# Grouped-query attention with a gated MLP, one decode step: slots at multiples of 512 bytes, the extra w_out rows on other DMA engines, the side table inside the MLP rows

## The chip, the cores and the metric

The kernel runs on one core of a Trainium2 chip. The time is the device time of one execution in microseconds (us); lower is better. A core has five instruction streams (PE for matmuls, DVE for vector work, ACT for activations, POOL, and SP, which here only issues DMAs) and sixteen DMA engines that carry all its transfers.

## The reference, cut to what matters

```python
xn = _layernorm(x)                                   # x: 8 x 1 x 512
q = (xn @ wq) ...                                    # 32 heads of 128
scores = einsum("bhqd,bhkd->bhqk", q, k) * (Dh ** -0.5)   # k_cache: 8 x 8 x 4096 x 128
o = einsum("bhqk,bhkd->bhqd", softmax(scores), v)    # v_cache: the same shape
s = o @ wo                                           # 4096 x 512
z = gelu(xn @ w_in); z1, z2 = z[:896], layernorm(z[896:])
g = silu((z1 * (w_sp * z2 + b_sp)) @ w_out)          # w_out: 896 x 512
return x + s * g
```

All is float32. The two caches are 134 MB each; each KV head serves four query heads. Nothing is reused across batches, so every byte of the caches is read once.

## The kernel before, in words

SBUF holds three large buffers, the slots of the pool `ring`: each is 128 partitions by 64 KB (8.4 MB). Everything large passes through them in turn. SP issues in this order: the MLP's weights into the first slot (`w_mlp`, L70, then three small transfers `w_low`, L75), `wq` into the second (L86), then for each of the 8 KV heads two halves of K (`load_k`, L313) and two halves of V (`load_v`, L320), one slot each, and around the last half of V the output weights `wo` in seven pieces (L324). A load into a slot waits on SP until the compute that read the slot's last content has ended. A full slot is one DMA with one row of 64 KB for each partition; an engine carries eight of them.

The pool `const` is allocated ahead of `ring` in each partition, so the sizes of its tiles set where the slots start. In this kernel the slots start at bytes 16,704, 82,240 and 147,776 of a partition.

**The MLP.** `w_out` has 896 rows, seven blocks of 128. Five of them (`MAIN`) lie in `w_mlp`, one row for each partition and block, and so come over all engines. The other two blocks, 1 and 3 (256 rows of 2 KB), come in the three transfers of the list `LOW`. An entry `(e, p0, c0, chunks)` is one DMA whose source has `e` outer rows and whose destination is `4 * e` partitions from `p0`, with the given chunks of w_out's rows side by side in the columns from `c0`. Each outer row of the source becomes four packets, one for each of its four partitions. In `mlp()` each chunk takes one transpose of the activations (L201), a DVE copy for all chunks of the same height in a group of up to four (L206), and matmuls (L215); entries at `p0 > 0` accumulate in the second PSUM bank.

**The start.** ACT issues `x` (8 rows of 2 KB, L64) and the side table (`side`, 128 rows of 520 bytes, L66: x in the layout of the output, and the two scalars w_sp and b_sp). DVE and POOL normalise x (L129 to L133), PE transposes it (L136), and the MLP's first matmuls (L155) wait for `w_mlp`. The scalars are read at L186, the copy of x by the last addition at L383.

**Attention.** For each head PE computes the scores of both halves of K (L258), softmax follows, and `values` multiplies by V (L300), with the reduction on DVE (L303, L305). At the end `wo` is multiplied as its pieces land (L331, L338), the result is gated and x added (L382, L383), and SP writes it out (L384).

Of the kernel before, what the change touches and what calls it, by code (L numbers as in the profile page):

```python
# [8 lines left out]
F32 = mybir.dt.float32  # L9
# [4 lines left out]
P = 128  # L14
B, D = 8, 512
HKV, REP, S, DH = 8, 4, 4096, 128
NK = D // P
G = 4
J = S // (G * P)
R = 32  # L20
FH = 896
# [12 lines left out]
MAIN = [0, 2, 4, 6, 5]  # L34


def rows_of(j, lo, hi, n):
    return [(j, r) for r in range(lo, hi, n)]


LOW = [(2, R, 2 * D, rows_of(3, 0, P // 2, 8)), (4, 0, 2 * D, rows_of(1, 0, P, 16)),
       (8, 0, 0, rows_of(3, P // 2, P, 32))]
LOW_COLS = 10 * D
HL_AT = [0, 0, 8]
HL_CH = 10


@with_exitstack
def tile_gqa_gmlp_decode(ctx: ExitStack, tc: tile.TileContext, x, side, kT, v, wq, wo,
                         w_mlp, lows, out):  # L50
    nc = tc.nc
    const = ctx.enter_context(tc.tile_pool(name="const", bufs=1))
# [3 lines left out]
    ps_fix = ctx.enter_context(tc.tile_pool(name="ps_fix", bufs=1, space=bass.MemoryType.PSUM))  # L56
    ps = ctx.enter_context(tc.tile_pool(name="ps", bufs=2, space=bass.MemoryType.PSUM))

    def slot():
        return ring.tile([P, SLOT], F32, name="slot")  # L60


    x_sb = const.tile([B, D], F32, name="x_sb")
    nc.scalar.dma_start(x_sb, x)  # L64
    side_sb = const.tile([P, P + 2], F32, name="side_sb")
    nc.scalar.dma_start(side_sb, side)  # L66

    mlp_slot = slot()
    n_in, n_mlp = NK * 2 * FH, NK * 2 * FH + len(MAIN) * D
    nc.sync.dma_start(mlp_slot[:, :n_mlp], w_mlp)  # L70
    w_in_sb = mlp_slot[:, :n_in].rearrange("p (k n) -> p k n", k=NK)
    low_sb = []
    for (e, p0, c0, chunks), w_low in zip(LOW, lows):
        t = mlp_slot[p0:p0 + e * LOW_R, n_mlp + c0:n_mlp + c0 + len(chunks) * D]
        nc.sync.dma_start(t, w_low[:, :LOW_R * len(chunks) * D].rearrange("e (i n) -> e i n", i=LOW_R))  # L75
        low_sb.append(t.rearrange("p (c d) -> p c d", d=D))
    w_out_sb = mlp_slot[:, n_in:n_mlp].rearrange("p (j d) -> p j d", d=D)
    spare = [n_mlp + LOW_COLS]

    def from_slot(rows, n):  # L80
        lo = spare[0]
        spare[0] = lo + n
        return mlp_slot[:rows, lo:lo + n]

    wq_sb = slot()
    nc.sync.dma_start(wq_sb, wq)  # L86
    wq_sb = wq_sb.rearrange("p (k n) -> p k n", k=NK)
# [49 lines left out]
    nc.vector.tensor_copy(xnT[:, :, :B], pt.rearrange("p (k b) -> p k b", k=NK))  # L137

    gate = const.tile([P, P], F32, name="gate")

    def mlp():
        zu = work.tile([P, 4, FQ], F32, name="zu", tag="p")
# [2 lines left out]
        hT = hy[:, :2 * P].rearrange("p (a s) -> p a s", a=2)  # L145
        hL = from_slot(P, HL_CH * P).rearrange("p (a s) -> p a s", s=P)
        y_sb, e = zu[:, :2].rearrange("p a f -> p (a f)"), zu[:, 2, :P]
# [45 lines left out]
        todo = [(0, hT[:, j % 2, R * (j // 2):R * (j // 2 + 1)], w_out_sb[:, i, :]) for i, j in enumerate(MAIN)]  # L193
        for (ne, p0, _, chunks), c0, w_low in zip(LOW, HL_AT, low_sb):
            n = ne * LOW_R
# [115 lines left out]
    def load_k(h, half):  # L311
        t = slot()
        nc.sync.dma_start(t, kT[h, half])  # L313
        return t.rearrange("p (i c g s) -> p i c g s", i=HALF, c=2, g=G)
# [65 lines left out]

    res = const.tile([P, P], F32, name="res")
    nc.vector.tensor_mul(res, acc, gate)  # L382
    nc.vector.tensor_add(res, res, side_sb[:, :P])  # L383
    nc.sync.dma_start(out, res)  # L384


# [43 lines left out]
```

## Time and profile before

| | |
|---|---|
| median of 3 runs | 684.03 us (683.95 to 684.05) |
| the profiled execution | 683.97 us |
| its span, first to last instruction | 682.2 us |
| busy: PE, DVE, ACT, POOL | 382.8, 170.5, 13.5, 3.9 us |
| mean rate read from HBM over the span | 426 GB/s |
| SP's DMA queue q1 | 6262 packets, 290.79 MB, 98.8% of 16 engines |
| instruction fetches, q8 and q14 | 20 packets with 0.33 MB, 3 with 0.02 MB |

The profile is of one execution, and its span is 1.8 us shorter than the time of the same execution. A row of waits names who ended an engine's idle time; a row of the chain gives a start, a length and what was being waited for, followed back from the last instruction. The trace also holds a record for every DMA packet: queue, start, length and bytes, but not the engine.

### The profile page before, as it was taken

How to read it: one execution, taken by the hardware profiler on the slowest of the kernel's cores; microseconds unless marked ns; L12 is line 12 of the kernel's file. 1: busy time of each engine (PE TensorE's matmuls, PEld its weight loads, DVE VectorE, ACT ScalarE, POOL GpSimd, SP SyncE). 2: the span in 40 equal slices, each digit the busy share in tenths (PEclk: the TensorE clock that was granted, in tenths of full speed). 3: DMA queues.
4: the chain of work that ended last, by engine and by line, in shares of the span. 5: the costliest groups of instructions: out<-in, count | busy, mean ns of one | idle time of the engine just before them, and what ended most of it. 6: DMA issues, size and time to landing. Idle time of an engine off the chain costs nothing.

```text
span 682.2 us, 5712 instructions
## 1 busy us (share of the span) xinstructions
PE 382.8 (56%) x2610; PEld 117.5 (17%) x2610; DVE 170.5 (25%) x272; ACT 13.5 (2%) x27; POOL 3.9 (1%) x11
## 2 busy tenths in 40 slices
PE   1488454456655355556754465655755356655666
PEld 0222121112111021111211021111211021111212
DVE  2531033401431024401431024401422024400432
ACT  0000000000000000000000000000000000000000
POOL 1000000000000000000000000000000000000000
PEclk9778667878767678887676678877667778876688
DMA  9999999999999999999999999999999999999996
GB/s 384 439 447 432 434 431 430 428 434 428 438 435 430 431 430 435 438 428 430 428 434 443 427 439 439 431 434 431 430 431 430 430 431 428 430 431 434 424 422 263
DMA packets 6445, 291.22 MB, mean 427 GB/s; under 512 B 726, under 2 KB 982, under 8 KB 1534
## 3 DMA queue, kind: packets, MB, share of 16 engines
q1 hardware_dynamic: 6262, 290.79, 98.8%
q8 instruction: 20, 0.33, 0.2%
q10 hardware_dynamic: 160, 0.08, 0.1%
q14 instruction: 3, 0.02, 0.0%
HBM read 290.80 MB, written 0.07 MB: 426 GB/s over the span
## 4 chain that ended last, share of the span: by engine, by line
DMA 79%; PE 16%; issue 4%; DVE 1%; POOLq 0%; POOL 0%
DMA slot<-in_kT 40%; DMA slot<-in_v 28%; DMA slot<-in_wo 10%; PE sc L258 8%; PE o_ps L300 6%; PE sc L215 1%; PE scr L201 0%; PE po_ps L309 0%; DMA x_sb<-in_x 0%; DVE zu L218 0%; DVE st L129 0%; PE scr L191 0%; POOLq L424 0%; POOL rstd L132 0%; PE sc L338 0%
## 5 line engine op out<-in xcount | busy, mean ns | idle before, releaser
L258 PE MATMUL sc<-slot,qz 128*32 128x512 f32 x1024 | 148.0, 743 | 132.1 <-DMA slot<-in_kT 132.1
L300 PE MATMUL o_ps<-slot,pT 128*16 128x512 f32 x1024 | 154.0, 744 | 77.8 <-DMA slot<-in_v 77.8
L303 DVE TENSOR_TENSOR o_all<-o_ps,diag 128x512 f32<-128x512 f32 x64 | 44.2, 691 | 156.7 <-PE o_ps L300 156.3
L263 DVE TENSOR_REDUCE nm<-sc 128x1 f32<-128x1024 f32 x8 | 9.8, 1224 | 278.7 <-PE sc L258 278.7
L258 PEld LDWEIGHTS sc<-slot,qz 128*32 128x32 f32 x1024 | 36.5, 133 | 237.3 <-DMA slot<-in_kT 138.1
L305 DVE TENSOR_REDUCE o_sb<-o_all 128x128 f32<-128x512 f32 x64 | 67.8, 1059 | 2.2
L300 PEld LDWEIGHTS o_ps<-slot,pT 128*16 128x16 f32 x1024 | 30.5, 113 | 161.6 <-issue 106.9
L309 PE MATMUL po_ps<-fold,o_sb 128*128 128x4 f32 x128 | 24.6, 263 | 24.1 <-DVE o_sb L305 23.8
L309 PEld LDWEIGHTS po_ps<-fold,o_sb 128*128 128x128 f32 x128 | 19.0, 188 | 68.8 <-DVE o_sb L305 65.5
L289 PE MATMUL scr<-ident,p 128*128 128x128 f32 x64 | 15.4, 422 | 10.7 <-DVE p L284 10.7
L265 ACT ACTIVATE p<-sc,nm 128x1024 f32<-128x1024 f32 x8 | 8.9, 1113 | 574.5 <-DVE nm L263 574.5
L289 PEld LDWEIGHTS scr<-ident,p 128*128 128x128 f32 x64 | 12.4, 221 | 11.1 <-issue 11.1
L290 DVE COPY pT<-scr 128x512 f32<-128x512 f32 x16 | 11.1, 691 | 11.3 <-PE scr L289 11.3
L155 PE MATMUL scr<-slot,xnT 128*32 128x256 f32 (+1 forms) x64 | 5.2, 464 | 9.5 <-DMA slot<-in_w_mlp 9.5
L236 PE MATMUL scr<-slot,xnT 128*32 128x512 f32 x64 | 9.4, 737 | 0.0
L268 PE MATMUL scr<-ident,nm 128*1 128x128 f32 x8 | 2.2, 270 | 10.9 <-DVE nm L263 10.9
L281 PE MATMUL scr<-wl,same 128*128 128x1 f32 x16 | 3.8, 309 | 6.2 <-DVE wl L279 6.2
L284 DVE TENSOR_SCALAR p<-p,w 128x1024 f32<-128x1024 f32 x8 | 6.0, 753 | 0.3
L331 PE MATMUL sc<-slot,oT 128*8 128x512 f32 x48 | 5.7, 593 | 0.2 <-DMA slot<-in_wo 0.2
L215 PE MATMUL sc<-slot 16*32 16x512 f32 (+2 forms) x36 | 5.3, 664 | 0.8 <-DVE zu L218 0.8
L171 PE MATMUL scr<-part_sum,same 128*128 128x1 f32 x4 | 1.1, 348 | 7.0 <-DVE part_sum L169 7.0
L155 PEld LDWEIGHTS scr<-slot,xnT 128*32 128x32 f32 x64 | 3.0, 141 | 11.3 <-issue 10.8
(87 smaller groups left out, 72.3 us busy)
## 6 DMA issues: line engine op xcount, KB each, us to landing
slot<-in_v SPq DMA_DIRECT2D x2, 4096.0 KB, 26.3
slot<-in_w_mlp SPq DMA_DIRECT2D x1, 4864.0 KB, 14.5
slot<-in_wo SPq DMA_DIRECT2D x1, 3072.0 KB, 36.5
slot<-in_wo SPq DMA_DIRECT2D x1, 2048.0 KB, 40.1
slot<-in_wo SPq DMA_DIRECT2D x1, 1280.0 KB, 42.7
slot<-in_wo SPq DMA_DIRECT2D x1, 768.0 KB
slot<-in_wo SPq DMA_DIRECT2D x1, 512.0 KB
slot<-in_wo SPq DMA_DIRECT2D x2, 256.0 KB, 31.8
```

The lines of the kernel that those rows point to most:

```text
L155: nc.tensor.matmul(pz[R * g:R * (g + 1), part * FQ:part * FQ + n], xnT[:, k, :], w_in_sb[:, k, part * FH + lo:part * FH + lo + n], start=( ...
L215: nc.tensor.matmul(sc[R * g:R * (g + 1), bank, :], lhsT, rhs, start=(i < G), stop=(i + G >= len(part)))
L236: nc.tensor.matmul(pq[R * g:R * (g + 1), :], xnT[:, k, :], wq_sb[:, k, lo:lo + REP * DH], start=(k == 0), stop=(k == NK - 1))
L258: nc.tensor.matmul(sc[R * g:R * (g + 1), c, :], qz[:, h, b * R:(b + 1) * R], k_sb[:, i, c, g, :], start=(b == 0), stop=(b == B - 1))
L263: nc.vector.tensor_reduce(m, sc, op=ALU.max, axis=AX.XY, negate=True)
L265: nc.scalar.activation(p.rearrange("p j s -> p (j s)"), sc.rearrange("p c s -> p (c s)"), AF.Exp, bias=m, accum_out=l[:, h:h + 1])
L289: nc.tensor.transpose(t[:, j * P:(j + 1) * P], p[:, 4 * c + j, :], ident)
L290: nc.vector.tensor_copy(pT[:, :, 4 * c:4 * c + 4].rearrange("p b j (g r) -> p (j g) b r", g=G), t.rearrange("p (m b r) -> p m b r", b=B, r ...
L300: nc.tensor.matmul(of[R * c:R * c + G * REP, :], pT[:, b, j, :], v_unit[:, j], start=(j < G), stop=(j >= J - G))
L303: nc.vector.tensor_mul(o_all, o, diag[:, :, None].to_broadcast([P, G, DH]))
L305: nc.vector.tensor_reduce(o_sb, o_all.rearrange("p g d -> p d g"), op=ALU.add, axis=AX.X)
L309: nc.tensor.matmul(po[:, b * REP:(b + 1) * REP], o_sb, fold, start=True, stop=True)
```

## The change

Four edits, with no change to the arithmetic:

- A tile `align` of 224 bytes a partition is put at the head of `const`; with the side table's tile gone and the tile `xg` added, the slots start at bytes 16,896, 82,432 and 147,968.
- `LOW` is divided anew: blocks 1 and 3 give 80 rows each as chunks of 20 rows to two transfers with five outer rows, and the remaining 96 rows as chunks of 12 to one transfer with three. `MAIN` is as before. There are 16 chunks where there were 18.
- The side table becomes 192 more columns of `w_mlp` (of which 130 are used), and its own transfer goes. POOL copies its 128 columns of x to `xg`, since the slot is overwritten later. The copy stands on POOL ahead of the power of the MLP's layer norm (L184).
- x is loaded in two halves of 256 columns.

```diff
-LOW = [(2, R, 2 * D, rows_of(3, 0, P // 2, 8)), (4, 0, 2 * D, rows_of(1, 0, P, 16)),
-       (8, 0, 0, rows_of(3, P // 2, P, 32))]
-LOW_COLS = 10 * D
-HL_AT = [0, 0, 8]
-HL_CH = 10
+LOW = [(5, 0, 0, rows_of(1, 0, 80, 20)), (5, 0, 4 * D, rows_of(3, 0, 80, 20)),
+       (3, R, 0, rows_of(1, 80, P, 12) + rows_of(3, 80, P, 12))]
+LOW_COLS = 8 * D
+HL_AT = [0, 4, 0]
+HL_CH = 8
+X_PARTS = 2
+ALIGN = 56
+SIDE = 192
...
+    const.tile([P, ALIGN], F32, name="align")
...
-    nc.scalar.dma_start(x_sb, x)
-    side_sb = const.tile([P, P + 2], F32, name="side_sb")
-    nc.scalar.dma_start(side_sb, side)
+    for c in range(0, D, D // X_PARTS):
+        nc.scalar.dma_start(x_sb[:, c:c + D // X_PARTS], x[:, c:c + D // X_PARTS])
...
-    n_in, n_mlp = NK * 2 * FH, NK * 2 * FH + len(MAIN) * D
+    n_in, n_mlp = NK * 2 * FH, NK * 2 * FH + len(MAIN) * D + SIDE
...
-    w_out_sb = mlp_slot[:, n_in:n_mlp].rearrange("p (j d) -> p j d", d=D)
+    side_sb = mlp_slot[:, n_mlp - SIDE:n_mlp]
+    w_out_sb = mlp_slot[:, n_in:n_mlp - SIDE].rearrange("p (j d) -> p j d", d=D)
...
+    xg = const.tile([P, P], F32, name="xg")
+    nc.gpsimd.tensor_copy(xg, side_sb[:, :P])
...
-    nc.vector.tensor_add(res, res, side_sb[:, :P])
+    nc.vector.tensor_add(res, res, xg)
```

On the host, `side` is laid out with 192 columns and appended to the rows of `w_mlp`.

More of the change, by code (lines that the diff above doesn't have):

```diff
@@ L38, in rows_of, with tile_gqa_gmlp_decode @@
     return [(j, r) for r in range(lo, hi, n)]
-LOW = [(2, R, 2 * D, rows_of(3, 0, P // 2, 8)), (4, 0, 2 * D, rows_of(1, 0, P, 16)),
-       (8, 0, 0, rows_of(3, P // 2, P, 32))]
-LOW_COLS = 10 * D
-HL_AT = [0, 0, 8]
-HL_CH = 10
+LOW = [(5, 0, 0, rows_of(1, 0, 80, 20)), (5, 0, 4 * D, rows_of(3, 0, 80, 20)),
[6 more added lines that the diff above has]
+SIDE = 192
 @with_exitstack
-def tile_gqa_gmlp_decode(ctx: ExitStack, tc: tile.TileContext, x, side, kT, v, wq, wo,
+def tile_gqa_gmlp_decode(ctx: ExitStack, tc: tile.TileContext, x, kT, v, wq, wo,
                          w_mlp, lows, out):
@@ L393 @@
     x = c(A_x).reshape(B, D)
-    side = np.zeros((G, R, P + 2), np.float32)
+    side = np.zeros((G, R, SIDE), np.float32)
     side[:, :B, :P] = x.reshape(B, G, P).transpose(1, 0, 2)
@@ L409 @@
         "x": x,
-        "side": side.reshape(P, P + 2),
         "kT": c(k.transpose(2, 0, 7, 1, 4, 6, 5, 3)).reshape(HKV, 2, P, SLOT),
@@ L416 @@
             c(B_w_in).reshape(NK, P, 2 * FH).transpose(1, 0, 2).reshape(P, NK * 2 * FH),
-            w2[MAIN].transpose(1, 0, 2).reshape(P, len(MAIN) * D)], axis=1),
+            w2[MAIN].transpose(1, 0, 2).reshape(P, len(MAIN) * D),
+            side.reshape(P, SIDE)], axis=1),
         **lows,
```

## The prediction, made before the changed kernel was run

> **What bounds the kernel now.** I read the page first (span, engines, queues, chain), then the chain of waits in order of time, then the timeline of the last microseconds, then the trace's DMA packet records one by one (start, length, bytes, queue), which no view prints. The page:
>
> ```profile
> span 682.2 us, 5712 instructions
> PE 382.8 (56%) x2610; PEld 117.5 (17%) x2610; DVE 170.5 (25%) x272; ACT 13.5 (2%) x27; POOL 3.9 (1%) x11
> ...
> DMA  9999999999999999999999999999999999999996
> ...
> q1 hardware_dynamic: 6262, 290.79, 98.8%
> q8 instruction: 20, 0.33, 0.2%
> q10 hardware_dynamic: 160, 0.08, 0.1%
> q14 instruction: 3, 0.02, 0.0%
> ```
>
> No compute engine passes 56%, and SP's queue q1 alone fills 98.8% of 16 DMA engines. The small rows matter too: q8 and q14 fetch instructions through the same engines. The chain:
>
> ```profile
> 542.78 9.48 PE sc L258 x64
> 552.27 0.02 issue
> 552.28 48.52 DMA slot<-in_kT
> 600.80 0.04 issue
> 600.84 9.47 PE sc L258 x64
> 610.31 0.02 issue
> 610.33 36.47 DMA slot<-in_wo
> 646.80 0.02 issue
> 646.82 31.85 DMA slot<-in_wo
> 678.66 0.04 issue
> 678.71 0.45 PE sc L338 x8
> ```
>
> PE's 9.5 us are only the time until a slot is free; the transfer then takes 48.5 us because two 8.4 MB loads are queued ahead of it. From 542.78 to 600.84 is 58.06 us for three loads, 433 GB/s, and every turn from 78 to 600 us repeats it within 0.01. So the end moves by as much as the slowest DMA engine finishes earlier or later. In the tail PE waits for the last pieces of wo by as little as 0.2 us:
>
> ```profile
> 674.27 1.04 PE L331 MATMUL sc<-slot,oT 128*8 128x512 f32 x8 [0.20 <-DMA slot<-in_wo]
> 677.40 0.41 PE L338 MATMUL sc<-slot,oT 128*8 128x128 f32 x8 [0.21 <-DMA slot<-in_wo]
> 678.71 0.41 PE L338 MATMUL sc<-slot,oT 128*8 128x128 f32 x8 [0.23 <-DMA slot<-in_wo]
> ```
>
> But PE's run up to there starts at the landing of the last half of v (666.28), which moves with the same engine, so a shift of all loads shifts all of it.
>
> **Who is the slowest engine.** The three w_low transfers leave 2, 4 and 8 completion packets of 4 bytes, so they ran on 2, 4 and 8 engines, and the extra packets identify groups: engines 0-1, 2-3, 4-7, 8-15. Following each group's completion packets through the 31 full slots (19.352 us each), the lag behind the first engine at 639 us is:
> - engines 0 and 1: 5.46 and 5.70 us, unchanged since 33 us. Their extra packets took 5.50 us each.
> - engines 2 and 3: 3.50 for one, 5.04 for the other, which took two 8 KB fetches of q14 at 0.97 each. Extra packets: 3.07.
> - engines 4-7: 0.68, 0.95 (1.68 after the third q14 fetch), 3.78, 3.94. Extra packets: 0.63.
> - engines 8-15: 0.07, 0.55 and six between 3.26 and 4.94.
> Each 16 KB fetch of q8 puts 1.55 us on one engine; they go round the same eight engines (two of 4-7, six of 8-15). So engine 0 or 1, at 5.70, sets the end: its last completion is at 678.21, the next PE row at 678.71.
>
> **Part 1, w_out rows.** Packet intervals (start to next start) in the records: 2 KB 81 ns, 4 KB 156, 16 KB 610, 64 KB 2417, a completion 6. The line through 2 KB and 64 KB is 27.18 bytes per ns plus 5.6 ns, so 8 KB is 307 ns. New load: two transfers of 4 packets of 8 KB on each of engines 0-4 (2 x (4 x 307 + 6) = 2.47 us), one of 4 of 16 KB on 0-2 (4 x 610 + 6 = 2.45).
> - Engines 0, 1: 4.91 instead of 5.50, -0.59: lag 5.11.
> - Engine 2: 4.91 instead of 3.07, +1.84: lag 5.34, or 6.88 if it is the one with the q14 fetches.
> - Engine 3: 2.47 instead of 3.07: 4.44 or 2.90. Engine 4: +1.83 on at most 1.68 (it is one of the two that q8 leaves alone, if q8's eight are neighbours): 3.5. Engines 5-7: -0.63. Engines 8-15 stay, at most 4.94.
> The q14 engine is 2 or 3. I take 3: the third q14 fetch falls on one of 4-7 that q8 does not use, and a row of neighbours (one per sequencer) that has DVE's fetches next to it gives 3 and 4. Then the slowest is engine 2 at 5.34: **-0.35 us**. Which of 0-2 is late in the first load (a spread of 0.76 us over engines) moves this between -0.06 and -0.76, the latter where the fetch engines at 4.94 take over.
>
> [...]
>
> **Part 2, alignment.** Slots start at byte 16,704 of a partition before (320 past a multiple of 512) and at 16,896 = 33 x 512 after. What a 64 KB packet takes over 27.18 bytes per ns is 2418 - 2411 = 7 ns (mean with its share of completions taken off), and that fixed part contains whatever the offset costs. An engine has 8 + 8 + 31 x 8 + 16 + 56 + 12 = 348 such packets, so the bounds are 0 and 7 x 348 = -2.4 us. A loss is hardly to be seen: all partitions share one offset before and after. Nearest row: the 4-byte completion, which never touches a slot, has a fixed part of 6 - 1 = 5 ns. I take the 2 ns above it: 2 x 348 = **-0.70 us**.
> [...]
>
> **Part 3, side table and x.** w_mlp grows by 768 bytes on 8 packets an engine: 8 x 28 = +0.23 us; the 8 side packets (28 ns, interval 25) and their completion go: -0.21. Two 1 KB packets of x instead of one of 2 KB, and a completion: +0.02 on engines 0-7. Sum **+0.03**. Nothing else reaches the path:
> - x lands when the second ACT issue does, about 0.6 us later (first issue 0.57 us); behind it on DVE stand bn_stats, the masks and xn, on POOL the power. xnT was ready at 6.07, PE begins L155 at 15.36: 9.3 us of cover, 0.6 without it.
> - The new POOL copy waits for w_mlp (15.3); behind it on POOL stands only the power of L184 (29.14). Its price lies between the POOL memset of 128x128 (0.20) and that of 128x2304 (2.02); cover 13.8 us. SP's second K load also waits for it, and waits for the whole MLP anyway.
> - The MLP loses 2 transposes, 4 PE rows of L215 and a DVE copy, so that K load goes out somewhat before 43.80. The engines have wq and the first K until 52.8, so it gains nothing (9 us).
> - SP's queue keeps its order and its 8 completion lanes (x's second half takes the place of side).
>
> **Sum.** -0.35 - 0.70 + 0.03 = -1.02. The profiled execution took 683.97 (span 682.2 and 1.8 around it), 0.06 under the median 684.03. So span 681.2, and 684.03 - 1.0 = **683.0 us**.
>
> **Rivals.**
> 1. *Alignment is worth most of the fixed part.* For: the bound itself. Against: completions cost nearly the same without it. At 3 to 7 ns a packet: -1.4 to -2.8 in all, 681.2 to 682.6. Its whole span counts as faster by over 0.2% (1.37 us, about what a measurement of this kernel can tell from no change). Chance 0.35.
> 2. *Engine 2 is the one with the q14 fetches.* Then engine 2 at 6.88 sets the end: +1.18, less alignment 0.70, plus 0.03: 684.5; without any alignment gain 685.2. It decides as soon as that engine's lag passes 5.70. For: group 2-3 alone is sure. Against: the neighbours. Chance 0.12, slower than before but mostly inside 0.2%.
> 3. *5 and 3 are no engine counts.* The trace shows 2, 4, 8 and 16 only. If such a transfer falls back to one engine, engine 0 gets 40 x 307 ns + 12 x 610 ns = 19.6 us instead of 5.5, +14.1 less 0.7 for alignment: 697.4, 2% slower. Chance 0.04. [...]
> The forecast, with up to 3 ns a packet, has 0.49.
>
> **Range.** Forecast -0.06 - 0 to -0.76 - 1.0: 682.2 to 684.0. Rival 1 down to 681.5 and rival 2 up to 684.6 leave out less than 2 in 10. Chances: faster by over 0.2% is rival 1 and the lower edge of the forecast, 0.38; slower by over 0.2% is rival 3 and the unaligned end of rival 2 with a bad first load, 0.08; the rest, 0.54, within.
>
> **What would show it.** Right: the w_low issues leave 5, 5 and 3 completions; a turn of three loads is 58.06 us less 24 x 2 ns = 58.01; 64 KB packets at 2415; the last engine's lag at 639 us about 5.3; PE's first L162 row near 15.4; last PE row 1.0 us earlier. Wrong: a turn at 58.06 (no alignment gain) or below 57.98 (rival 1), a lag near 6.9 on an engine with q14 fetches (rival 2), any idle DMA slice.

## The result, and the profile after

The changed kernel takes 682.25 us (median; 682.10 to 682.34) against 683.98 for the kernel before beside it (683.80 to 684.12): ratio 0.9974, 95% interval 0.9967 to 0.9982. It is 1.73 us faster, where 1.0 was forecast (683.0); the range 681.5 to 684.6 holds it. The gain is a quarter of a per cent, just over the 0.2% that the likeliest case stayed within; it lies at the lower edge of the forecast (682.2 to 684.0), in the stretch that the prediction had also given to its first rival (681.2 to 682.6).

The page of the changed kernel, the rows that answer to those shown of before:

```profile
span 680.3 us, 5701 instructions
PE 379.6 (56%) x2604; PEld 116.5 (17%) x2604; DVE 170.2 (25%) x271; ACT 13.5 (2%) x27; POOL 4.2 (1%) x12
...
DMA  9999999999999999999999999999999999999996
...
q1 hardware_dynamic: 6257, 290.88, 99.0%
q8 instruction: 20, 0.33, 0.2%
q10 hardware_dynamic: 32, 0.02, 0.0%
q14 instruction: 3, 0.02, 0.0%
```

SP's queue q1 is still the whole of the time, with slightly more bytes; ACT's queue q10 has lost the 128 side packets and their completions. The span fell by 1.9 us (680.3 against 682.2), the profiled executions by 1.87 (682.10 against 683.97). The chain of waits, start, length and what was waited for:

```profile
512.44 48.18 DMA slot<-in_v
560.62 0.14 issue
...
570.47 48.11 DMA slot<-in_kT
618.58 0.04 issue
618.62 8.66 PE sc L265 x64
627.29 0.02 issue
...
627.69 36.85 DMA slot<-in_v
664.53 0.04 issue
664.58 6.07 PE o_ps L307 x32
...
676.85 0.45 PE sc L345 x8
677.29 0.03 issue
677.32 0.30 DVE res L389
```

The turn of three loads, from one landing to the landing three slots later, is 618.58 - 560.62 = 57.96 us, where it was 58.06; below 57.98 was the prediction's sign for its first rival. The chain goes through the slots in another order and ends differently: after the last half of V lands (664.53; PE had begun on it at 666.28 before) PE itself shows no idle time for wo any more. The rows of before with 0.20 to 0.23 us of waiting for in_wo have become runs of PE work; only the weight load (PEld) for the last piece still waits for it:

```profile
673.04 1.04 PE L338 MATMUL sc<-slot,oT 128*8 128x512 f32 x8
...
676.21 1.04 PE L345 MATMUL sc<-slot,oT 128*8 128x128 f32 x24
676.85 0.12 PEld L345 LDWEIGHTS sc<-slot,oT 128*8 128x8 f32 x8 [0.30 <-DMA slot<-in_wo]
```

So in the tail PE and the last piece of wo are level, and PE's run up to there starts at the landing of V.

**Where the 1.7 us lie.** From the trace's DMA packet records, the completions of the slowest engine in queue q1:

| stretch | before | after | difference |
|---|---|---|---|
| to its completion of wq (the start, w_mlp, w_low, wq) | 39.16 us | 38.68 us | -0.48 |
| the next 31 full slots | 599.89 | 598.88 | -1.00 |
| the rest (halves of V, pieces of wo) to the last completion | 39.17 | 38.94 | -0.23 |
| last completion | 678.21 | 676.50 | -1.71 |

A full slot takes 19.351 us before and 19.319 after, 32 ns less for 8 packets: 4.0 ns a packet. The lag of the slowest engine behind the first one in the same load fell from 5.63 to 5.07 us at the last full slot (the prediction counts its lags from a point 0.07 us earlier: its 5.70 is this 5.63).

### The profile page after: what moved, and what is told of

Its sections match the earlier page's. It is cut to its first block, busy times and chain, and to the rows that moved or that the text cites. A ratio compares the mean times of both kernels' runs of the same rounds, so it can differ in the third digit from the quotient of the medians.

```text
span 680.3 us, 5701 instructions
## 1 busy us (share of the span) xinstructions
PE 379.6 (56%) x2604; PEld 116.5 (17%) x2604; DVE 170.2 (25%) x271; ACT 13.5 (2%) x27; POOL 4.2 (1%) x12
## 4 chain that ended last, share of the span: by engine, by line
DMA 77%; PE 18%; issue 2%; DVE 2%; POOLq 0%; SPq 0%; POOL 0%
DMA slot<-in_v 40%; DMA slot<-in_kT 35%; PE o_ps L307 7%; PE sc L265 7%; DMA slot<-in_w_mlp 2%; PE scr L243 1%; PE sc L222 1%; DVE o_sb L312 1%; PE po_ps L316 1%; PE scr L208 1%; PE sc L338 0%; DVE o_all L310 0%; PE sc L345 0%; DVE q_sb L246 0%; DVE part_sb L381 0%
## 5 line engine op out<-in xcount | busy, mean ns | idle before, releaser
L265 PE MATMUL sc<-slot,qz 128*32 128x512 f32 x1024 | 144.6, 728 | 132.4 <-DMA slot<-in_kT 132.4
L222 PE MATMUL sc<-slot 20*32 20x512 f32 (+1 forms) x32 | 5.6, 823 | 0.8 <-DVE zu L225 0.8
```

What stands on the lines that cost most here:

```text
L222: nc.tensor.matmul(sc[R * g:R * (g + 1), bank, :], lhsT, rhs, start=(i < G), stop=(i + G >= len(part)))
L265: nc.tensor.matmul(sc[R * g:R * (g + 1), c, :], qz[:, h, b * R:(b + 1) * R], k_sb[:, i, c, g, :], start=(b == 0), stop=(b == B - 1))
```

## The experiments

Each edit ran beside the kernel before on the same chip, so its ratio is what to compare.

| kernel | us | before beside it | ratio, interval | us a full slot (slowest engine) |
|---|---|---|---|---|
| changed kernel | 682.25 | 683.98 | 0.9974 (0.9967 to 0.9982) | 19.319 |
| align_only | 682.63 | 683.86 | 0.9982 (0.9973 to 0.9991) | 19.325 |
| rows_only | 683.62 | 683.86 | 0.9998 (0.9989 to 1.0007) | 19.351 |
| align_rows | 682.40 | 684.07 | 0.9974 (0.9963 to 0.9984) | 19.319 |
| side_x | 684.19 | 684.00 | 1.0002 (0.9993 to 1.0010) | 19.351 |
| x_one | 682.20 | 684.00 | 0.9972 (0.9961 to 0.9984) | 19.319 |
| off256 | 682.14 | 683.86 | 0.9976 (0.9966 to 0.9985) | 19.320 |
| off192 | 683.73 | 684.07 | 0.9994 (0.9985 to 1.0003) | 19.351 |
| off128 | 683.45 | 683.86 | 0.9995 (0.9986 to 1.0004) | 19.360 |
| off32 | 684.00 | 684.07 | 0.9998 (0.9989 to 1.0007) | 19.359 |
| four | 683.60 | 684.07 | 0.9993 (0.9984 to 1.0002) | 19.357 |
| all16 | 683.18 | 684.00 | 0.9987 (0.9978 to 0.9996) | 19.444 |
| six | 683.86 | 684.00 | 0.9999 (0.9990 to 1.0008) | 19.446 |

(The last column is a mean over 31 slots and also holds what the last engine lost to instruction fetches and other disturbances on the way. In align_only 26 of the 31 took 19.318 to 19.319 us and five lost up to 0.08.)

### One part at a time

**align_only**: the kernel before with a tile that moves the slots.

```diff
+    const.tile([P, 48], F32, name="align")
```

> The kernel before, with nothing but a tile of 192 bytes ahead in its constants, so that the slots start at 16,896 (33 x 512). Theory A (alignment is worth 4 ns on each of 348 packets, as the packet intervals of the changed kernel suggest: 2414 instead of 2418 for 64 KB): 683.98 - 1.35 = 682.6, period of a full slot 19.319 us, and the two engines with 147 KB of extra rows still the last, 5.7 us behind. Theory B (alignment is worth the 2 ns of the prediction and the start or the rows gave the rest): 683.3.

Measured 682.63, -1.23 us: theory A. Engines 0 and 1 are still the last (5.36 and 5.43 us behind).

**rows_only**: the kernel before with the new `LOW`, `LOW_COLS`, `HL_AT` and `HL_CH`.

> The kernel before with the new list of w_out rows alone; slots stay at 320 past a multiple of 512, side table and x as before. Theory A: the slowest engine's extra packets go from 5.50 to 4.91 us, its lag from 5.70 to 5.1 to 5.35, so -0.35 to -0.6: 683.4 to 683.65, period still 19.351. Theory B: -0.9 or more, 683.1 or less.

Measured 683.62, -0.24 us, at the small end of theory A but inside the interval of no change, so this run alone does not show a gain. Its runs lie near 683.6 (seven) and near 684.0 (four); the profiled execution took 683.92, and in it one of engines 0 to 2 came out of the first load 0.82 us after the first engine and is the last one all the way (5.75 behind, the next 5.12). Theory B fell with both runs.

**align_rows**: both together, the side table still in its own transfer and x whole.

> The kernel before with the aligned slots and the new list of w_out rows, but the side table in its own transfer and x whole. Alignment alone gave 0.9982 and rows alone 0.9998 of the kernel before. If these two parts are the whole change (side table and x are worth nothing, as side_x alone said), the ratio is that of the changed kernel, 0.9974 +- 0.0004. If the side table inside w_mlp has a share once the slots are aligned, it stays at 0.9978 to 0.9980.

The ratio is that of the whole change (682.40, -1.67 us). Alignment and rows make up the change as far as an interval of 0.001 (0.7 us) to either side can tell.

**side_x**: the side table in `w_mlp` and x in halves, the slots kept at 320 past a multiple of 512.

```diff
-LOW = [(5, 0, 0, rows_of(1, 0, 80, 20)), (5, 0, 4 * D, rows_of(3, 0, 80, 20)),
-       (3, R, 0, rows_of(1, 80, P, 12) + rows_of(3, 80, P, 12))]
+LOW = [(2, R, 2 * D, rows_of(3, 0, P // 2, 8)), (4, 0, 2 * D, rows_of(1, 0, P, 16)),
+       (8, 0, 0, rows_of(3, P // 2, P, 32))]
...
-ALIGN = 56
+ALIGN = 136
```

(the diff is against the changed kernel; the three column constants go back with `LOW`)

> The kernel before with the side table inside w_mlp and x in two halves alone; slots kept at 320 past a multiple of 512 by a larger align tile, w_out rows as before. The prediction gave this part +0.03: 684.0 beside a kernel before at 683.98 (683.9 beside 683.86), within the interval of no change. If instead the parts add up to the whole, what is left of -1.73 after -1.23 (alignment alone) and -0.24 (rows alone) lies here: -0.26, 683.6 to 683.7. x's second half should land near 8 us, as in the changed kernel, without anything waiting longer than for w_mlp.

No change that can be told (1.0002). The remainder of 0.26 us that I looked for did not show up here. Alignment and rows measured apart add up to -1.47 us, together they gave -1.67 and the whole change -1.73; each of these is known to about 0.6 us, so where the difference lies stays open.

**x_one**: the changed kernel with `X_PARTS = 1`.

> The changed kernel with x in one transfer again. If the late second half of x (bn_stats starts at 8.04 instead of 2.86) lies under the wait for w_mlp, the time stays at 682.2 and only bn_stats moves back to about 2.9; if it was on the path, 1 us or more comes off.

The time stays (682.20). What moves is the start of bn_stats; the timeline of the changed kernel, then of x_one:

```profile
8.04 0.68 DVE L134 BATCH_NORM_STATS2 st<-x_sb 8x6 f32<-8x512 f32 x1 [6.09 <-DMA x_sb<-in_x]
11.05 0.19 DVE L142 COPY xnT<-scr 128x32 f32<-128x32 f32 x1
15.39 1.08 PE L162 MATMUL scr<-slot,xnT 128*32 128x256 f32 x9 [4.37 <-DMA slot<-in_w_mlp]
```

```profile
2.54 0.68 DVE L134 BATCH_NORM_STATS2 st<-x_sb 8x6 f32<-8x512 f32 x1 [0.60 <-DMA x_sb<-in_x]
5.55 0.19 DVE L142 COPY xnT<-scr 128x32 f32<-128x32 f32 x1
15.57 1.03 PE L162 MATMUL scr<-slot,xnT 128*32 128x256 f32 x6 [10.06 <-DMA slot<-in_w_mlp]
```

The last bracket is the idle time before the row and what ended it. With x in two halves PE waits 4.4 us for w_mlp, with one transfer 10.1: the second half ate more than half of the cover, and nothing else.

### How much alignment is enough

`ALIGN` in the changed kernel is set to 120 (slots at 256 past a multiple of 512), 104 (192), 88 (128) and 64 (32).

> The changed kernel with its slots at 256 past a multiple of 512 (the align tile 256 bytes larger). If the cost comes with pieces of 256 bytes, this costs nothing: 682.25 and a period of 19.319. If it comes with pieces of 512, the 4 ns a packet return: 683.6 and 19.351.

> The changed kernel with its slots at 128 past a multiple of 512. If only multiples of 256 (or 512) are free and any other offset costs the same: 683.6, period 19.351. [...] If 128 is enough: 682.25.

> The changed kernel with its slots at 192 past a multiple of 512. Theory: any start off a multiple of 256 bytes costs about the same, so 683.4 to 683.6 and 2418 ns a packet, as at 64 and 128 past. [...]

> The changed kernel with its slots at 32 past a multiple of 512. Same theory: 683.4 to 683.6. [...]

256 is as good as 512. The times of 192 and 128 are 683.73 and 683.45, close to what was expected; 32 is at 684.00, above the 683.4 to 683.6 expected, though by the time alone it can't be told from 192. The records tell them apart. Lengths of the 4096 packets of 64 KB in each profile (leaving out the 20 or 21 that took over 2.5 us), and what the last engine took for a full slot in the median:

| slot start past a multiple of 512 bytes | mean ns | share of packets at 2418 ns or less | us a full slot, median |
|---|---|---|---|
| 0 | 2418.2 | 96% | 19.319 |
| 256 | 2418.3 | 95% | 19.319 |
| 128 | 2421.2 | 32% | 19.348 |
| 192 | 2421.5 | 16% | 19.350 |
| 320 (kernel before) | 2421.5 | 13% | 19.350 |
| 32 | 2422.3 | 7% | 19.358 |

Two things follow. The cost is not the same in every packet: off the boundary 7 to 32% of the packets take 2418 ns or less like the aligned ones, and most of the others 2419 to 2428. And it does not grow with the distance from the boundary below: 32 bytes past it cost the most (2422.3 ns), 128 the least of the four (2421.2). The boundary of 256 is what the runs show (2418.2 and 2418.3 ns at 0 and 256); where this order comes from they do not.

### Which engines the extra rows lie on

The diffs are against the changed kernel; the old lines of `LOW`, `LOW_COLS`, `HL_AT` and `HL_CH` are left out.

**all16**: all of w_out in `w_mlp`, nothing in `LOW`.

```diff
-MAIN = [0, 2, 4, 6, 5]
+MAIN = [0, 2, 4, 6, 5, 1, 3]
...
+LOW = []
+LOW_COLS = 0
+HL_AT = []
+HL_CH = 8
```

> The changed kernel with all seven blocks of w_out in w_mlp, so that every DMA engine carries 16 KB of each and no transfer runs on fewer than 16. [...] By the trace, the eight engines that fetch PE's instructions are then last, 3.0 to 5.0 us behind from their fetches plus 1.23: slower than the changed kernel by 0.8 to 1.1 us, 683.0 to 683.3.

683.18, as expected from the trace (the 1.23 us is a quarter of the 4.91 us on engines 0 to 2, for 32 KB instead of 128), and 0.9 us slower than the changed kernel, although after wq all engines lay within 0.61 us of each other (5.17 in the changed kernel). During the 31 full slots the eight engines that queue q8's fetches fall on went to between 2.8 and 4.3 us behind. (That q8 is PE's is an estimate: PE has 5208 of the changed kernel's 5701 instructions, and q8 makes 20 of the 23 fetches in its span.)

**four**: all extra rows on engines 0 to 3.

```diff
+LOW = [(4, 0, 0, rows_of(1, 0, P, 16)), (4, R, 0, rows_of(3, 0, P, 16))]
+HL_AT = [0, 0]
```

> The changed kernel with all 256 extra rows on DMA engines 0 to 3, 128 KB each (4.87 us): engines 0 to 2 carry what they carry in the changed kernel, engine 3 twice what it did, engine 4 nothing. If engine 3 is the one that takes the two 8 KB fetches of q14 (0.83 us each with aligned slots), it is last with 4.9 + 1.7 us and its place in the first load (0 to 0.7): 1.4 to 2.0 us slower than the changed kernel, 683.6 to 684.2. If these fetches cost the loads nothing, the time stays at 682.2.

683.60. One engine, 4.87 us behind after wq, took the two q14 fetches (0.84 and 0.83 us) and ended 6.39 behind, the next 5.24. PE waits for the last pieces of wo again:

```profile
676.98 0.41 PE L344 MATMUL sc<-slot,oT 128*8 128x128 f32 x8 [0.16 <-DMA slot<-in_wo]
678.28 0.41 PE L344 MATMUL sc<-slot,oT 128*8 128x128 f32 x8 [0.22 <-DMA slot<-in_wo]
```

**six**: an attempt at a better version, 240 rows on engines 0 to 5.

```diff
+LOW = [(6, 0, 0, rows_of(1, 0, 120, 24) + rows_of(3, 0, 120, 24)),
+       (1, R, 0, rows_of(1, 120, P, 4) + rows_of(3, 120, P, 4))]
+LOW_COLS = 10 * D
+HL_AT = [0, 0]
+HL_CH = 10
```

> The changed kernel with 240 of the 256 rows on DMA engines 0 to 5 (80 KB each, 3.0 us) and the last 16 rows on engine 0 (1.2 us). Engines 0 to 2 then lie at 3.0 to 4.9, engine 3 with its two fetches at 4.7 to 5.3, and the fetch engines at up to 5.0 are next: the last engine moves by 0 to -0.3, so 681.9 to 682.25. If the fetch engines were not the floor, engines 0 to 2 alone would give -0.7 or more: 681.5.

A miss: 683.86, with runs from 683.31 to 685.43. The profile is of an execution of 685.30. In it one of the engines 0 to 5 takes 16 KB fetches (at 40, 300 and 576 us) and is 8.00 us behind at the last full slot, the next 5.13. The last turns of the chain:

```profile
572.71 49.08 DMA slot<-in_kT
621.78 0.04 issue
621.83 8.72 PE sc L265 x64
630.55 0.02 issue
...
630.94 36.71 DMA slot<-in_v
667.65 0.04 issue
```

The last half of V lands at 667.65 where it landed at 664.53, and the whole tail follows. In the changed kernel no engine of the groups 0 to 2 and 3 to 4 took such a fetch, so the one here is engine 5, if the fetches use the same eight engines in both kernels. That the executions differ by 2 us would fit a round of eight that begins at another engine each time, so that engine 5 takes two fetches or three; only one execution was profiled, so this stays open. Nor was the entry with one outer row confined to engine 0: it left four completions, so it ran on four engines, one packet each.

## Why the prediction was right, and where it was off

**The bound: right.** In every profile here the span ends 3.8 to 4.1 us after the slowest engine of queue q1 has finished its last load; a change that moved neither its packets' length nor its load moved nothing (side_x 684.19 beside 684.00, x_one 682.20 where the changed kernel takes 682.25).

**w_out rows (-0.35): right in mechanism; the size fits, but rests on the records of single executions.** 8 KB packets have an interval of 306 ns (307 was taken) and 16 KB 607. From the table of stretches, of the 0.48 us by the end of wq, 28 packets at 4 ns are an estimated 0.11; the other 0.37 is this part with the side table. The two last engines, 5.07 us behind, are of engines 0 to 2, the third of these is at 4.84, and one of the fetch engines is at 4.88: rows taken off engines 0 to 2 could have gained no more than another 0.2 us. The time of rows_only alone (-0.24) can't be told from no change.

**Engine 3, not 2 (rival 2): settled.** Before, the engine with the two q14 fetches was one of the two that the transfer on four engines had and the one on two had not, so 2 or 3; after, it is one of 3 or 4. Only 3 fits both, if these fetches stay on one engine from kernel to kernel, and `four` shows the price of loading it (6.39 us behind, the next 5.24). That the fetch engines lie in a row, one for each sequencer, and that q14 is DVE's, was an assumption that no run shows. Rival 3 fell too: the transfers left 5, 5 and 3 completions.

**Engines 5 to 7 and 4: one wrong step.** I took q8's eight engines for neighbours that leave 4 and 5 alone. `six` points to a fetch engine at 5 (8.00 us behind after three 16 KB fetches). It cost the forecast nothing, since the change takes rows away from engine 5, but in the profiled execution it is why the better version failed.

**Alignment (-0.70): right in sign, half the size.** This is the term that was mis-sized: 348 packets at 2 ns were predicted. Measured are 4.0 ns on the 248 packets of the full slots (1.00 us) and 0.23 us on the 72 of the rest; with the estimate for the start that is 1.3 us, and align_only gave 1.23. The step that failed is the nearest row. I held the packet's fixed part (7 ns) against that of a 4-byte completion (5 ns) and called the rest the cost of the offset. But the completion was no floor (where it is written no record shows): aligned, a 64 KB packet takes 2414 ns, 3 over the 2411 of the line, less than a completion's 5. Nor was the cost a constant that sits in each packet: in the records of before the 64 KB packets had lengths of 2418, 2420 and 2427 side by side, and I read that spread as noise. Aligned packets are 95% at one value. Nor did the cost grow with the packet from 16 KB on: the median interval fell from 609 to 607 ns for 16 KB, from 1212 to 1209 for 32 KB and from 2417 to 2414 for 64 KB. What makes the cost stays open. Rival 1 had the size (3 to 7 ns a packet) with a chance of 0.35; that the time still fell on the edge of the forecast's own stretch is luck, since that stretch was held open for a larger gain of the rows (up to 0.76 us) than came.

**Side table and x (+0.03): right in sum, wrong in one step.** x's second half was to land 0.6 us later; bn_stats starts 5.2 us later (8.04 against 2.86). In the records the second half's eight packets of 1 KB lie at 5.34 to 6.07 and their completions at 6.85 to 7.58: the pieces start as w_mlp packets end that had begun at 3.85 us and later, and their completions as the next ones end, and a w_mlp packet takes 1.46 us or more. That fits two queues that take turns packet by packet on each engine; the records do not name the engine. I had priced the issue on ACT and not the queue behind it. The cover of 9.3 us held. The new POOL copy took 0.29 us.

**The tail: right that it moves with V**; PE's waits of 0.20 to 0.23 us for the last pieces of wo are gone, and the weight load for the last piece, released at 676.85, shows that PE and wo are level there.

## What to carry to other kernels

In a kernel bound by DMA like this one (q1 at 99.0% of 16 engines), look at each engine's own queue and not at the mean: what set the end here was one engine's bytes plus the instruction fetches that fell on it (in `four`, the engine 4.87 us behind after wq took two fetches, 0.84 and 0.83 us, and ended 6.39 behind, the next 5.24), so extra bytes go on engines that few fetches use. Start large SBUF buffers at a multiple of 256 bytes; here that took a full slot of eight 64 KB packets from 19.351 to 19.319 us (0.17%) and cost a dummy tile. And a small transfer issued behind a large one on another queue waited here for whole packets of it (with x's second half bn_stats starts at 8.04 us, with x in one piece at 2.54), so what is needed early goes out first and in one piece.

## What the runs showed of the hardware that I had not expected

- A slot start off a multiple of 256 bytes cost 3 to 4 ns on a 64 KB packet by its mean length (2421.2 to 2422.3 ns against 2418.2; 3.6 to 4.9 by the time of a full slot), as a spread (most at 2418 to 2428 ns) and not as a constant; 32 bytes off was the dearest of the four such offsets tried (2422.3 ns).
- Instruction fetches got cheaper with alignment too: a 16 KB fetch of q8 put 1.55 us on its engine before and 1.41 after, one of 8 KB on q14 0.97 and 0.84; the fetch packets themselves took 1064 ns in the mean before, 933 after and 927 in align_only.
- An engine that took a 16 KB fetch lost 1.55 us before and 1.41 after, over twice the interval of a 16 KB packet of a slot (610 ns before, 607 after). Why was not tried.
